# A state-space scan and a two-layer block on one Trainium2 core: reordering the first two pairs of chunks

## The chip, the cores and the metric

One core of a Trainium2 chip runs the whole program. The metric is device time in microseconds of one execution; lower is better. The span that a profile gives is some 1.7 us shorter than the time that is reported for the same execution (380.2 against 381.91 us for the profiled run of the kernel before); it runs from the first to the last instruction. All runs below were in the fast state, and all gave the correct result.

## The reference, cut to what matters

A selective state-space scan over 4 batches, 8 heads, 768 steps, 32 values and 16 states per head; its output, as 3072 tokens of 256 values, goes through two matrices with a leaky activation between them.

```python
# a clipped to [1e-6, 1]; the state runs from step to step of a sequence
M      = (C @ B.T) * causal * prod(a[j+1..i])     # inside a chunk
y      = M @ x + (C @ state) * prod(a[..i])       # "running products" of a
state  = prod(a) * state + B.T @ (x * prod(a[j+1..]))
# then, token by token
h = y @ w_in                                      # 256 -> 2048, 16 steps f of 128
g = max(h, 0) + alpha * min(h, 0)
out = g @ w_out                                   # weights come as float64
```

The weights arrive as 64-bit floats and are converted on the chip, tile by tile (512 KB raw each): ScalarE takes a part (`wt`, `wg`), GpSimd a limit on `wt`, VectorE two bit operations (`wr`), and GpSimd, or VectorE with it, the closing addition into `w_in` or `w_out`.

## The kernel before: the parts that the change touches

The kernel works on chunks of 128 steps in pairs (256 tokens). Pairs 0 and 1 are one group of 512 tokens. The first four hidden steps (f=0 to 3) of this group are done in halves, as soon as a pair is there; from f=4 on, all 512 tokens are there and the long steady stretch begins. An operation that waits holds those behind it on its engine: in the change SyncE waited 3.9 us for one transfer, until 11.76 us, and issued no other load in that time (below). To *spread* the decays is to have TensorE copy their rows to all 128 partitions. *Warming products* (`keep_warm`) are matmuls on a constant tile whose results nobody uses; they keep TensorE busy in a wait (in the kernel before, four of them, eight matmuls, take 1.73 us ahead of pair 1's output products).

```python
    # pair 0: decays z spread by TensorE, running products pf by VectorE
    if gp == 0:
        z = first_a(ap, nc.vector)
        ahead[0] = spread(z, 0)
        nc.vector.tensor_scalar(out=ap, in0=ap, ...)            # clamp
        pf = prep.tile([P, 2 * Q], F32, name="pf")
        for k in range(2):
            nc.vector.tensor_tensor_scan(out=pf[:, ks], data0=ap[:, ks], data1=zeros, ...)
    ...
    # the order of the loads on SyncE's queue
    load_next(2)                    # weight tiles 1 and 2
    held["pr"] = rows_scan(0)
    rows_out(0)                     # stores of the rows: z and pf
    load_next()                     # weight tile 3
    load_pair(1)
    load_second()                   # pair 1's running products
    load_next(3)                    # tiles 4 to 6
    load_pair(2)                    # with its spread decays, 2 x 512 KB
    # convert_next() issues the load of tile 7 and of the later ones
    ...
    prelus = [hidden_two(0, 0, spare())]        # f=0, 1, first 256 tokens
    convert_a(*pieces[2])                       # ScalarE's and GpSimd's part of tile 3
    convert_next()                              # closing addition of tile 2
    ssm(1)
    prelus.append(hidden_two(0, 2, bank(0)))    # f=2, 3: needs tile 2
    ...
    for f in range(FIRST):                      # second 256 tokens, one f at a time
        hidden(0, f, 2 * Q, 2 * Q)
        if f == 1:
            identity_bank()
        if f % 2:
            convert_next()
```

## Time and profile before

| | kernel before |
|---|---|
| time, median (range) at first | 381.88 us (381.42 to 383.98), 3 runs |
| time, medians in the five later sets of runs | 380.98 to 381.47 us |
| mean granted TensorE clock, profiled run | 0.998 |
| output products of pair 0 start | 15.67 us |
| hidden products of f=0 / f=2 start | 18.01 / 23.53 us |
| hidden products of f=4 (512 tokens) start | 34.64 us |
| VectorE starts its part of f=4 | 40.03 us |

The prediction, further down, reads the engine table, the busy time by stretch and the chain of work of this kernel. Three more readings of the same trace are used there: ScalarE's table load took 1.28 us, from 6.01 us; pair 1's Gram bank for GpSimd took a ScalarE copy of 0.61 us (at 23.44) and a GpSimd product of 1.27 us (at 24.95); and a DMA packet of 1 KB took 46 ns in the median (640 packets in the first 60 us), so 128 of them, spread over 16 engines, come to some 0.4 us (an estimate from this figure). Three lines of TensorE's timeline are added here, since the comparison rests on them. Columns: start and length in us, engine, source line, operation, output and inputs, shapes, count; in square brackets the idle time just before and what is taken to have ended it.

```profile
15.67 0.37 PE L579 MATMUL ss<-cd,sm 64*128 64x128 f32 x1
...
18.01 1.90 PE L620 MATMUL hp<-xT,w_in 128*128 128x256 f32 x8
...
23.53 1.99 PE L620 MATMUL bank<-xT,w_in 128*128 128x256 f32 x8 [0.87 <-POOL w_in L247]
```

The first is the start of pair 0's output products (`cd` is C times the running products, `sm` the masked state). The second is the first hidden product. The third, for f=2, waited 0.87 us for GpSimd's closing addition of the second weight tile; remember that wait.

### The profile page before, as it was taken

The numbers are of one execution on the slowest core, as the hardware profiler recorded it, in microseconds if no ns is written. First come the engines' busy times: TensorE is split into PE (matmuls) and PEld (weight loads), VectorE is DVE, ScalarE is ACT, GpSimd is POOL, SyncE is SP. The second block draws the span as 40 slices with busy tenths as digits, with TensorE's granted clock in tenths as the row PEclk, the third lists the DMA queues.
The fourth block names the chain that finished last, engine by engine and source line by source line (L and its number), as shares of the span: only waits on it lengthen the run. The fifth ranks groups of instructions, "written<-read, shape, count | busy, mean of one in ns | idle before, by whom it ended". The sixth has DMA issues, their size and how long they took to land.

```text
span 380.2 us, 6170 instructions
## 1 busy us (share of the span) xinstructions
PE 371.0 (98%) x2223; PEld 294.8 (78%) x2223; DVE 241.2 (63%) x462; ACT 178.0 (47%) x384; POOL 200.3 (53%) x210
## 2 busy tenths in 40 slices
PE   8998999999999999999999999999999999999995
PEld 7775566668888788788788788788788788888884
DVE  6994799968537637738737747637847644643363
ACT  2575765525354444454444445445435425553441
POOL 4565465778858744634645535455445356254511
PEclk9999999999999999999999999999999999999999
DMA  7989897721008701004603603703701001001003
GB/s 143 195 216 300 212 290 161 154 68 57 28 21 174 138 3 55 2 0 69 140 2 62 146 2 57 152 0 54 154 2 28 2 0 28 3 0 29 0 0 83
DMA packets 121877, 30.71 MB, mean 81 GB/s; under 512 B 93736, under 2 KB 117752, under 8 KB 121848
## 3 DMA queue, kind: packets, MB, share of 16 engines
q1 hardware_dynamic: 116736, 29.74, 35.1%
q10 hardware_dynamic: 5112, 0.59, 1.1%
q8 instruction: 17, 0.28, 0.3%
q14 instruction: 12, 0.10, 0.1%
HBM read 26.98 MB, written 3.34 MB: 80 GB/s over the span
## 4 chain that ended last, share of the span: by engine, by line
PE 85%; DVE 4%; DMA 4%; SPq 2%; ACT 1%; issue 1%; POOL 1%; ACTq 0%; POOLq 0%; DVEq 0%
PE hp L728 34%; PE bank L703 32%; PE bank L642 5%; PE hp L606 4%; PE ss L586 2%; PE ss L534 2%; DMA nat<-in_C_dram 2%; DMA raw<-in_moe_w_in_dram 2%; PE ss L579 1%; DVE dec L421 1%; PE ss L505 1%; PE hp L534 1%; PE ss L450 1%; SPq L158 1%; DVE wr L241 1%; SPq L156 1%
## 5 line engine op out<-in xcount | busy, mean ns | idle before, releaser
L771 POOL TENSOR_TENSOR gt<-gt 128x512 f32<-128x512 f32 x58 | 73.7, 1271 | 25.9 <-DVE gt L713 17.8
L703 PE MATMUL bank<-gt,w_out 128*128 128x256 f32 x320 | 82.4, 381 | 0.0
L713 DVE SCALAR_TENSOR_TENSOR gt<-hp,s_mul,gt 128x256 f32<-128x256 f32 x120 | 52.5, 479 | 41.5 <-ACT gt L711 40.7
L711 ACT ACTIVATE gt<-hp,s_alpha 128x256 f32<-128x256 f32 x120 | 50.3, 470 | 48.0 <-PE hp L728 37.3
L762 POOL TENSOR_TENSOR gt<-gt 128x512 f32<-128x512 f32 x20 | 25.4, 1272 | 86.7 <-DVE gt L713 86.7
L703 PEld LDWEIGHTS bank<-gt,w_out 128*128 128x128 f32 x320 | 60.2, 190 | 10.2 <-issue 2.3
L703 PE MATMUL bank<-gt,ws 128*128 128x256 f32 x240 | 61.4, 379 | 0.0
L703 PEld LDWEIGHTS bank<-gt,ws 128*128 128x128 f32 x240 | 45.1, 190 | 5.8
L421 DVE TENSOR_TENSOR_SCAN dec<-abc,bank 128x256 f32<-128x256 f32 x80 | 48.1, 660 | 0.0
L747 DVE TENSOR_TENSOR hp<-hp,u 128x512 f32<-128x512 f32 x20 | 14.0, 700 | 49.1 <-ACT u L745 49.1
L728 PE MATMUL hp<-xT,w_in 128*128 128x256 f32 x160 | 43.1, 392 | 0.2
L728 PE MATMUL hp<-xs,w_in 128*128 128x256 f32 x160 | 43.1, 392 | 0.1
L728 PE MATMUL hp<-xs,ws 128*128 128x256 f32 x160 | 41.1, 379 | 0.0
L736 ACT COPY m<-hp 128x512 f32<-128x512 f32 x20 | 11.7, 586 | 57.4 <-PE hp L728 52.9
L728 PEld LDWEIGHTS hp<-xT,w_in 128*128 128x128 f32 x160 | 28.7, 189 | 9.1 <-ACT hp L757 4.7
L728 PEld LDWEIGHTS hp<-xs,w_in 128*128 128x128 f32 x160 | 28.4, 189 | 8.8 <-issue 4.2
L728 PEld LDWEIGHTS hp<-xs,ws 128*128 128x128 f32 x160 | 30.4, 190 | 4.1
L642 PEld LDWEIGHTS bank<-w_out,gt 128*128 128x128 f32 x128 | 24.2, 190 | 8.9 <-issue 5.4
L642 PE MATMUL bank<-w_out,gt 128*128 128x256 f32 x128 | 30.8, 381 | 0.0
L606 PE MATMUL hp<-xT,w_in 128*128 128x512 f32 (+1 forms) x64 | 27.2, 553 | 1.3 <-DVE gt L610 1.0
L751 DVE TENSOR_TENSOR c<-hp,m 128x512 f32<-128x512 f32 x20 | 13.6, 682 | 19.2 <-PE hp L728 19.2
L745 ACT COPY u<-hp 128x512 f32<-128x512 f32 x20 | 11.7, 586 | 19.6 <-PE hp L728 18.4
(157 smaller groups left out, 547.0 us busy)
## 6 DMA issues: line engine op xcount, KB each, us to landing
abc<-z SPq DMA_DIRECT2D x20, 512.0 KB, 5.7
raw<-in_moe_w_in_dram SPq DMA_DIRECT2D x8, 512.0 KB, 5.4
raw<-in_moe_w_out_dram SPq DMA_DIRECT2D x8, 512.0 KB, 5.8
xt<-in_x_dram SPq DMA_DIRECT2D x24, 128.0 KB, 2.9
out_dram<-o_sb SPq DMA_DIRECT2D x32, 64.0 KB, 1.9
nat<-in_B_dram SPq DMA_DIRECT2D x22, 64.0 KB, 2.7
nat<-in_C_dram SPq DMA_DIRECT2D x22, 64.0 KB, 3.4
ap<-pf SPq DMA_DIRECT2D x11, 128.0 KB
```

The costliest lines, as they stand in the source:

```text
L421: nc.vector.tensor_tensor_scan(out=dv[:, k, hs], data0=abc[k][:, hs], data1=ident_p[0], initial=0.0, op0=ALU.mult, op1=ALU.add)
L606: nc.tensor.matmul(hp, w_in[:, k, f * P : (f + 1) * P], xts[g][:, k, t0 : t0 + nt], start=(k == 0), stop=(k == KC - 1))
L642: nc.tensor.matmul(pos[0][t // 2][:, t % 2], gt[:, t * Q : (t + 1) * Q], w_out[:, f], start=(f == 0 and t % 2 == 0), stop=(f == NF - 1), s ...
L703: nc.tensor.matmul(ms[g][i][:, h], w, blocks[g, z][n][:, p], start=(q == 0 and h == 0), stop=(q == NQ - 1), skip_group_check=True)
L711: nc.scalar.mul(o[:, p], h[:, p], s_alpha[:, fs[p]])
L713: nc.vector.scalar_tensor_tensor(out=o[:, p], in0=h[:, p], scalar=s_mul[:, fs[p]], in1=o[:, p], op0=ALU.mult, op1=ALU.max)
L728: nc.tensor.matmul(to[:, p], w(2 * z + p), b, start=start and p == 0, stop=True, skip_group_check=True)
L736: nc.scalar.copy(out=m1, in_=A)
L747: nc.vector.tensor_tensor(out=Y, in0=Y, in1=u2, op=ALU.add)
L751: nc.vector.tensor_tensor(out=c22, in0=A, in1=m5, op=ALU.add)
L762: nc.gpsimd.tensor_tensor(out=tc_, in0=g22, in1=g12, op=ALU.subtract)
L771: eng.tensor_tensor(out=o, in0=x0, in1=x1, op=ALU.subtract)
```

## The change

Its intent is to shorten the front: VectorE is relieved of the clamp and two scans of pair 0 (the running products come back by a load from the store that is made anyway), one of four banks of Gram products goes to GpSimd, the decays are spread before the rows' work, the second 256 tokens of f=0 to 3 are done two steps to a bank, and the weight tiles are loaded in twos between the pairs' loads.

```diff
@@ pair()
         if gp == 0:
             z = first_a(ap, nc.vector)
             ahead[0] = spread(z, 0)
-            nc.vector.tensor_scalar(out=ap, in0=ap, scalar1=1e-6, scalar2=1.0, ...)
-            pf = prep.tile([P, 2 * Q], F32, name="pf")
-            for k in range(2):
-                ...tensor_tensor_scan(out=pf[:, ks], data0=ap[:, ks], data1=zeros, ...)
+            ahead[1] = spread(z, 1, bank)
             loads["z", 1] = first_a(loads["a", 1], nc.gpsimd)
+            yield
+            pf = first_pf
+            turned = rows_turn(0, held.pop("pr"))
... (cut: tiles and warming products; half of pair 0's `cz` from ScalarE to
...  GpSimd; pair 1's second spread moved ahead of the hidden products of f=0)
         if gp == 0:
             gram = products_bc()
-            dps = added()
+            dps = added(spare())
             yield
+            c_decayed()                                # GpSimd
+            times(dec[:, :, :2], one_less(gram))       # ScalarE copy, GpSimd product
@@ rows_out()
-            nc.sync.dma_start(out=scratch[key, i], in_=t)
+            eng = nc.scalar if (key, i) == ("pf", 0) else nc.sync
+            eng.dma_start(out=scratch[key, i], in_=t)
@@ order of the loads
     load_next(2)
+    first_pf = prep.tile([P, 2 * Q], F32, name="pf")
+    rows_clamp(0)
+    ssm(0)
     held["pr"] = rows_scan(0)
     rows_out(0)
-    load_next()
+    load_products(0, first_pf)
     load_pair(1)
-    load_second()
-    load_next(3)
-    load_pair(2)
+    load_products(1, loads["p", 1][3])
+    load_next(2)
+    load_pair(2, False)
+    load_next(2)
+    load_spread(2, *divmod(4, CPB))
@@ order of the work
+    convert_a(*pieces[2])
+    convert_next(first=False)                  # tile 2's addition, still behind tile 3
     ssm(1)
-    prelus.append(hidden_two(0, 2, bank(0)))
+    convert_a(*pieces[3])
+    prelus.append(hidden_two(0, 2, 0, spare()))
...
-    for f in range(FIRST):
-        hidden(0, f, 2 * Q, 2 * Q)
-        if f == 1:
-            identity_bank()
-        if f % 2:
-            convert_next()
+    convert_next(first=False)
+    for rest in [hidden_two(0, f, 2 * Q, spare()) for f in range(0, FIRST, 2)]:
+        rest()
+    identity_bank()
+    convert_a(*pieces[5])
+    convert_next()
```

## The prediction

> **What bounds the kernel now.** I read the engine table, then busy time by stretch, then the chain of work that ended last. TensorE is busy 98% of the 380.2 us span:
>
> ```profile
> PE 371.0 (98%) x2223; PEld 294.8 (78%) x2223; DVE 241.2 (63%) x462; ACT 178.0 (47%) x384; POOL 200.3 (53%) x210
> ```
>
> The busy time by stretch puts PE at 99.94 of 100 us from 100 to 200 us and 99.86 from 200 to 300. The change touches only the first two pairs of chunks and the first four f-steps, which end at 34.6 us when the first 128x512 hidden product starts. So only the start can be shortened, and PE's idle time in the first 60 us (5.2 us in these stretches) bounds the gain loosely. Transfers by stretch:
>
> ```profile
> 8.00:13.00 5.00, 4.79 (x58) 3.58 (x59) 4.29 (x6) 3.54 (x9) 1.99 (x3) 1.00 1.03 331
> 13.00:16.00 3.00, 2.65 (x20) 1.97 (x18) 2.90 (x7) 0.77 (x2) 1.35 (x2) 1.00 0.67 84
> 16.00:24.00 8.00, 6.94 (x90) 5.18 (x87) 7.45 (x11) 6.13 (x13) 5.01 (x10) 1.00 1.03 260
> 24.00:29.00 5.00, 4.91 (x56) 3.85 (x54) 4.38 (x9) 2.28 (x6) 3.28 (x5) 1.00 0.69 86
> 29.00:40.00 11.00, 9.79 (x37) 6.57 (x38) 4.34 (x8) 7.20 (x17) 5.86 (x7) 1.00 1.02 325
> 40.00:60.00 20.00, 19.08 (x89) 12.15 (x87) 19.11 (x34) 13.28 (x23) 11.01 (x12) 1.00 0.85 233
> ```
>
> The last two columns are the busy share of the DMA engines and GB/s. DMA is saturated from 8 to 40 us but for two holes: 13 to 16 us loses 3 x 0.33 = 1.0 us, 24 to 29 us loses 5 x 0.31 = 1.55 us. From 40 to 60 us VectorE is the full engine (19.11 of 20). The chain says how these join:
>
> ```profile
> 10.13 3.28 SPq L158
> ...
> 13.45 1.63 SPq L156
> ...
> 15.12 2.68 DMA nat<-in_C_dram
> 17.80 0.04 issue
> 17.84 0.33 PE hp L450
> ...
> 22.21 1.28 POOL w_in L247
> ...
> 25.53 1.73 PE bank L256 x8
> ...
> 29.57 7.12 DMA raw<-in_moe_w_in_dram
> ```
>
> Pair 1's C arrives at 17.80 us, its conversion of weights ends at 23.49, four wasted warming products fill 1.73 us, and from 29.57 the chain leaves PE for a weight transfer: the seventh raw weight tile (call it raw7), which lands at 36.69. ScalarE waits for it in order, with the work of step f=4 behind it, and VectorE behind that:
>
> ```profile
> 36.77 0.68 ACT L213 ACTIVATE wt<-raw 128x512 f32<-128x512 f32 x1 [2.43 <-DMA raw<-in_moe_w_in_dram]
> 40.03 0.75 DVE L610 SCALAR_TENSOR_TENSOR gt<-hp,s_mul,gt 128x512 f32<-128x512 f32 x1 [3.57 <-ACT gt L609]
> ```
>
> From 40.03 VectorE has no gap until 50.4, where PE waits for it; after 61 us PE alone is the chain. So the end moves with VectorE's start at 40.03, that is with raw7, and PE's 5 us do not count in full.
>
> [...] the store of the decay rows (z), issued from SP at 7.51 us behind two 512 KB weight tiles, has its landing event only at 11.87, against a median of 2.3 us for such stores.
> [...] The granted clock here is 1.00 in every stretch[...].
>
> **The change part by part.**
>
> *Spread ahead of the rows.* VectorE now clamps `ap` right after the rows' clamp instead of after two scans; `ap` has its landing event at 3.76 us, so z is ready near 4.25 instead of 5.17. Seven warming products instead of ten end at 1.23 + 14 x 0.217 = 4.3 us. The spread starts near 4.65 instead of 5.80. VectorE's first decay scan follows 1.5 us later, as now: 6.15 instead of 7.30. The four scans take 4 x 1.15 us and end near 10.8 instead of 12.19. *Gain so far 1.35 us.*
>
> *Running products by a load.* VectorE loses a clamp and two scans (0.29 + 0.89 us). In return the products make a round trip through DRAM. The store moves to ScalarE's queue, where it waits for nat C (7.43 us), ahead of the table load. It lands near 9.2 to 9.8 (2.3 us for such a store). The load of 128 KB follows behind the two weight tiles and lands near 12.6. Two costs: the table load no longer fills idle time but runs 7.9 to 9.2, then two copies, so `bc` ends at 10.2 instead of 9.36; and GpSimd's `cd` waits until 12.6 instead of running at 9.44.
>
> *Gram bank by GpSimd.* VectorE loses 0.65 us, ScalarE gains a 0.61 copy, GpSimd 1.27. GpSimd then runs `cd` 12.6 to 13.3, the product to 14.7, the mask to 15.4 (0.73 each for first and last). VectorE, with the first weight conversion (0.41 + 0.69) moved forward, ends its last gram near 15.0. So pair 0's output products start near 15.6, now 15.67: *the 1.35 us is spent on GpSimd's chain, nothing is left of it here.*
>
> *Pair 1.* Its loads go out behind two weight tiles instead of three, and C should land near 16.7 instead of 17.80. Transposes 17.0 to 18.0; spread to 19.2 (now after the hidden products); hidden_two to 20.95; sums and grams to 22.9. GpSimd ends the second weight conversion near 24.1, because ScalarE reaches the third tile's part later (now 23.49): hidden_two 24.15 to 26.0. Two warming products instead of four save 0.86 us; output products 26.9 to 28.35, now 27.25 to 28.73. *Gain 0.35 us.*
>
> *Tokens two to a bank.* Now eight products of 128x256 run from 29.18 to 34.64 through two buffers, each waiting for ScalarE and VectorE: 5.46 us, of which PE needs about 3.6 and the transposes 0.6. In pairs they should need 28.8 to 33.0. *Gain 1.3 us more, 1.65 in all at step f=4.*
>
> *Loads reordered.* Before raw7 the same bytes move as now, plus the 128 KB (0.4 us: 128 packets x 50 ns / 16 engines). What changes are the holes. Now SP is blocked for 3.28, 1.63, 2.28, 3.15 and 1.54 us at small transfers behind three weight tiles, and issues the next ones after DMA has run dry. With tiles in twos the small transfers go out while the tiles still run. If both holes (2.5 us) close and 0.4 + 0.4 us (product load, round trip) are added, raw7 lands near 36.7 - 2.5 + 0.8 = 35.0; if half closes, near 36.2. ScalarE itself, by its order, is free for raw7 near 34.8 (pair products until 32.6, a bank copy 0.38, the sixth tile 1.8).
>
> *Sum.* VectorE starts f=4 near 35.0 + 3.3 instead of 40.03: -1.7 us; PE is ready for it by -1.65. Behind it the order on all engines is unchanged, so the end moves by -1.6 us; half-closed holes give -0.5.
>
> **The rivals.**
> (A) *DMA keeps raw7 where it is.* For it: 1.02 of share from 29 to 40 us, the same bytes, and one weight tile fewer ahead of pair 1, so one more after. Against: the holes. Time then 381.5 to 382.3; PE would reach f=4 early and stand at f=6.
> (B) *GpSimd's chain in pair 0 or the third weight tile is worse than I think.* The product load is a new wait, and ScalarE needs the third tile near 21.5, while it lands near 20. Two microseconds late there would make 382 to 383.
> (C) *The front gains more.* If the product load lands by 11.5, pair 0 gains another 1 us and, holes closed, VectorE's start moves by 2.5 us or more: 378.5 to 379.5.
> (D) *PE falls to half clock* with fewer warming products. The first matmul of 0.58 us against 0.27 later hints at it; PE is fuller than now, so I give it little.
>
> **Range and chances.** Centre 381.9 - 1.6 = 380.3 us. (A) and (B) together bound it above near 382.0, (C) below near 378.5; I take these as the 8 in 10. A 2% change is 7.6 us, more than all of PE's idle time in the front, so faster by 2% is nearly out. Slower by 2% would need a stall of over 7 us, which no wait I found approaches. Chances 0.02, 0.97, 0.01.
>
> **What would show it.** First decay scan near 6.2 us and the fourth ending near 10.8 (step 1). `cd` of pair 0 waiting for DMA until about 12.6, and pair 0's output products still near 15.6. Hidden_two for f=2 starting near 24. First 128x512 hidden product near 33.0 (now 34.6). ScalarE's wait for raw7 ending near 35.0 and VectorE's gap ending near 38.3; DMA share above 0.9 in 13 to 16 and 24 to 29 us. From 61 us on all stretches as now, only shifted. I am wrong if raw7 lands at 36.5 or later and the total is still shorter (then the chain through it is no bound), or if the front moves by 3 us and the end by none.

## The result, and the profile after

The changed kernel took 386.59 us in the median of 4 runs (385.79 to 388.11), the kernel before 382.00 of 4 runs (381.42 to 383.98). The ratio is 1.0121, with a 95% interval from 1.0075 to 1.0167. Ratios here and below are the mean time of one kernel's fast runs over that of the other's fast runs of the same rounds, so not quite the ratio of the quoted medians. The change makes the kernel 1.2% slower; 380.3 us had been predicted, in a range from 378.5 to 382.0, and the measured median lies 4.6 us above the top of the range.

The page of the changed kernel already shows one difference. Each digit of this line is the granted TensorE clock of one fortieth of the span, in tenths; it was 9 throughout before.

```profile
PEclk9879999999999999999999999999999999999999
```

The busy time by stretch, with the stretches of the prediction. Columns: stretch, its length, busy time (and count) of PE, PEld, DVE, ACT and POOL, granted clock, DMA share, GB/s.

```profile
8.00:13.00 5.00, 4.67 (x49) 3.69 (x51) 4.49 (x6) 4.35 (x10) 2.21 (x3) 1.00 0.64 211
13.00:16.00 3.00, 1.80 (x18) 1.23 (x14) 2.20 (x5) 1.11 (x2) 1.08 (x2) 1.00 0.73 108
16.00:24.00 8.00, 6.22 (x57) 4.88 (x58) 5.27 (x6) 2.24 (x5) 5.22 (x10) 0.58 0.98 217
24.00:29.00 5.00, 3.37 (x32) 2.31 (x30) 4.12 (x7) 3.19 (x7) 1.91 (x4) 1.00 0.87 132
```

From 16 to 24 us the clock was 0.58: half speed from 17.22 to 24.05 us, and TensorE was nearly as busy as before (6.22 against 6.94 us) for far fewer matmuls (57 against 90). From 8 to 13 us DMA fell from a share of 1.03 to 0.64. Two waits lie behind both. The chain of work of the changed kernel (start, length, what):

```profile
12.23 2.65 issue
...
14.92 0.45 POOL cd L486
...
15.60 1.26 POOL dec L568
16.86 0.87 POOL sm L542
...
17.77 0.58 PE ss L609
```

GpSimd's `cd` could start only at 14.92 us; its product and its mask follow in order; and the output products of pair 0 start at 17.77 us, not at 15.67. What `cd` and TensorE waited for is in their timelines (first GpSimd, then TensorE):

```profile
14.92 0.72 POOL L486 TENSOR_TENSOR cd<-bc,pf 128x256 f32<-128x256 f32 x1 [2.69 <-DMA pf<-pf]
```

```profile
17.77 0.58 PE L609 MATMUL ss<-cd,sm 64*128 64x128 f32 x1 [2.97 <-POOL sm L542]
```

The load of the running products landed at 14.84 us. It was issued at 11.76 us, when the store had landed (11.75), and SyncE had issued nothing since 7.78 us, with all loads of pair 1 still to come. This is the longest of SyncE's own waits (us in total, times, longest):

```profile
SPq L176 <- DMA pf<-rpf: 3.9, 1, 3.9
```

So one round trip costs three things: 2.10 us on GpSimd's chain, a hole of 3.9 us in the issue of loads, and a gap of 2.97 us on TensorE (14.80 to 17.77 us), in which the clock fell to half (at 17.22). At half clock the first product took 0.58 us here, at full clock 0.37 in the kernel before.

Taken point by point, in us from the start:

| | before | predicted | change |
|---|---|---|---|
| first decay scan | 7.30 | 6.15 | 6.63 |
| fourth decay scan ends | 12.19 | 10.8 | 11.20 |
| load of the running products lands | none | 12.6 | 14.84 |
| pair 0's output products start | 15.67 | 15.6 | 17.77 |
| hidden products of f=0 start | 18.01 | - | 23.42 |
| hidden products of f=2 start | 23.53 | 24.15 | 29.31 |
| hidden products of f=4 start | 34.64 | 33.0 | 38.09 |
| seventh weight tile lands (last of its landing events) | 36.69 | 35.0 | 38.62 |
| VectorE starts f=4 | 40.03 | 38.3 | 43.75 |
| span | 380.2 | - | 384.1 |

VectorE's start moved by 3.72 us and the span by 3.9: the loss lies ahead of that start. The span less that start is 340.17 us before and 340.35 after; in all 17 profiles of this study it lies between 340.1 and 341.3.

In the changed kernel nobody waits for the seventh tile any more. ScalarE comes to it late, with its own work in a row:

```profile
38.59 0.38 ACT L333 COPY bank<-ident_h 128x256 f32<-128x256 f32 x1
38.89 0.68 ACT L218 ACTIVATE wt<-raw 128x512 f32<-128x512 f32 x1
39.46 1.15 ACT L228 ACTIVATE wg<-raw,g_add,g_mul 128x256 f32<-128x256 uint16 x2
40.49 0.68 ACT L218 ACTIVATE wt<-raw 128x512 f32<-128x512 f32 x1
```

The reader is to see no bracket in the last line: the seventh tile is there when ScalarE reaches it, 1.9 us after its last landing event at 38.62 us.

### The profile page after: what moved, and what is told of

It is laid out like the page before. It is cut to its first block, busy times and chain, and to the rows that moved or that the text cites. A ratio compares the mean times of both kernels' runs of the same rounds, so it can differ in the third digit from the quotient of the medians.

```text
span 384.1 us, 6169 instructions
## 1 busy us (share of the span) xinstructions
PE 371.9 (97%) x2221; PEld 296.1 (77%) x2221; DVE 241.3 (63%) x458; ACT 178.0 (46%) x384; POOL 202.5 (53%) x212
## 3 DMA queue, kind: packets, MB, share of 16 engines
q1 hardware_dynamic: 116760, 29.82, 35.4%
## 4 chain that ended last, share of the span: by engine, by line
PE 87%; DVE 5%; ACT 3%; issue 2%; ACTq 1%; POOL 1%; DMA 1%; POOLq 0%; DVEq 0%
PE hp L759 34%; PE bank L734 31%; PE bank L673 5%; PE hp L635 3%; PE ss L616 3%; PE hp L650 2%; PE ss L556 2%; PE ss L609 1%; DVE dec L440 1%; PE ss L527 1%; PE hp L556 1%; PE ss L466 1%; DVE wr L239 1%; DMA nat<-in_C_dram 1%; DVE gt L639 1%
## 5 line engine op out<-in xcount | busy, mean ns | idle before, releaser
L635 PE MATMUL hp<-xT,w_in 128*128 128x512 f32 x48 | 23.2, 605 | 0.0
```

The source lines that it names most:

```text
L635: nc.tensor.matmul(hp, w_in[:, k, f * P : (f + 1) * P], xts[g][:, k], start=(k == 0), stop=(k == KC - 1))
```

## The experiments

The first theory was that the products' round trip is the cause, through its wait and the half clock. Its rivals were the order of the loads, the order of the conversions, and that the half clock is only a sign of waiting. Each set of runs has its own runs of the kernel before on the same chip (medians 381.23, 380.98, 381.19, 381.47 and 381.36 us), and each ratio is to those.

| run | what is different | ratio (95%) | median us | VectorE starts f=4 |
|---|---|---|---|---|
| change | | 1.0121 (1.0075 to 1.0167) | 386.59 | 43.75 |
| E1 | change, products by VectorE | 1.0087 (1.0061 to 1.0113) | 384.35 | 41.90 |
| E2 | change, gap at pair 0 filled | 1.0111 (1.0091 to 1.0131) | 385.28 | 42.75 |
| E3 | change, tiles 1, 2 behind the round trip | 1.0127 (1.0104 to 1.0150) | 386.07 | 44.61 |
| E4 | before, second tokens two to a bank | 0.9998 (0.9982 to 1.0013) | 381.34 | 39.14 |
| E5 | E1, old loads | 1.0029 (1.0017 to 1.0042) | 382.33 | 40.66 |
| E6 | E1, conversions swapped | 1.0084 (1.0053 to 1.0116) | 384.45 | 38.88 |
| E7 | E1, old loads and conversions swapped | 1.0007 (0.9997 to 1.0017) | 381.21 | 38.77 |
| E8 | change, old loads and conversions swapped | 1.0062 (1.0043 to 1.0082) | 383.07 | 41.04 |
| E9 | before, tile 7 ahead of pair 2's spread decays | 0.9987 (0.9969 to 1.0005) | 380.28 | 37.78 |
| E10 | E7, tile 7 first, tile 6 earlier on ScalarE | 0.9926 (0.9900 to 0.9952) | 378.33 | 35.78 |
| E11 | E4, tile 7 first, tile 6 earlier on ScalarE | 0.9952 (0.9937 to 0.9968) | 379.47 | 37.41 |
| E12 | change, old loads | 1.0119 (1.0088 to 1.0151) | 385.63 | 43.65 |
| E13 | change, conversions swapped | 1.0103 (1.0076 to 1.0131) | 385.02 | 42.23 |
| E14 | change, both gaps filled | 1.0123 (1.0088 to 1.0157) | 385.86 | 43.65 |
| E15 | change, old loads and the gap at pair 0 filled | 1.0079 (1.0057 to 1.0100) | 384.32 | 41.45 |

Two cautions go with this table. The ratio of the change comes from 4 runs and is known to some 0.5% only. E5, E7 and E8 are clear of it; the single repairs E1, E2, E3, E12 and E13, and E14, E6 and E15, are not told from it by the timed ratio alone, so for these the traces carry the argument. And each start in the last column is from one execution. The traced one of the kernel before took 381.91 us, 0.4 to 0.9 us above the later medians; with 1.7 us off for the span and 340.2 us after the start, those medians put its usual start near 39.1 to 39.6 us (an estimate), not at 40.03.

### E1: the products by VectorE again

```diff
-    load_products(0, first_pf)
+    first_ap = loads["p", 0][3]
+    nc.vector.tensor_scalar(out=first_ap, in0=first_ap, scalar1=1e-6, scalar2=1.0, ...)
+    for k in range(2):
+        ...tensor_tensor_scan(out=first_pf[:, ks], data0=first_ap[:, ks], data1=zeros, ...)
```

> The changed kernel with one thing undone: VectorE forms pair 0's running products again (a clamp and two scans, 1.2 us, placed in its gap before the first decay scan), so nothing of pair 0 waits for the round trip through DRAM; the store stays on ScalarE's queue and pair 1 still loads its products. If the wait for the loaded products is the cause (theory W), pair 0's output products start near 15.2 us instead of 17.8, PE's idle stretch of 3 us before them is under 0.7 us, the clock is never granted at half from 17 to 24 us, step f=4 starts near 33 us instead of 38.1 and the kernel takes 379.5 to 381.5 us, at least 5 us less than the change. If the new order of the loads or the gram bank on GpSimd is the cause, it stays at 384 us or more.

Pair 0's output products started at 16.02 us (17.77 in the change), and there was no half clock at 17 us. Yet the time was 1.0087: about a quarter of the loss came back, if any (the intervals overlap), and the expected 5 us did not. ScalarE's timeline shows a new wait, for the fifth weight tile, with the copies of pair 1's output (`xT`) behind it, for which the second tokens' hidden products wait:

```profile
30.69 0.68 ACT L218 ACTIVATE wt<-raw 128x512 f32<-128x512 f32 x1 [1.43 <-DMA raw<-in_moe_w_in_dram]
31.27 0.66 ACT L225 ACTIVATE wg<-raw 128x512 f32<-128x512 uint16 x1
31.82 0.37 ACT L623 COPY xT<-bank 128x256 f32<-128x256 f32 x1
```

In the old order the fifth tile goes out ahead of pair 2's loads, in the new one behind them. In the change it landed at 31.47 us and ScalarE reached it at 32.07, so the wait was hidden by only 0.6 us.

### E2: the gap at pair 0 filled with warming products

```diff
-            keep_warm(y[0].rearrange("p k t -> p (k t)"), 2)
+            keep_warm(y[0].rearrange("p k t -> p (k t)"), 8 if gp == 0 else 2)
```

> The changed kernel with eight warming products instead of two ahead of pair 0's output products, which fill PE's idle stretch while the products are on their way. The wait stays, so the output products still start near 17.8 us. If the half clock from 17.2 to 24.0 us is a cause of its own (theory C), it goes away and PE gets back up to half of these 6.8 us: output products 0.9 us, transposes 0.5, spread 1.1, hidden_two 0.3: 2.8 us, so about 384 us. If the clock costs nothing at the end, the time stays within 0.5 us of the change.

The fill worked where it stood: no half clock from 17 to 24 us, and the hidden products of f=0 began at 20.92 instead of 23.42 us, though pair 0's output products began at 17.81 as in the change. But the clock then fell at the end of the next gap (1.94 us), ahead of f=2, and was half from 26.4 to 29.8 us, and ScalarE waited 0.49 us for the fifth tile. VectorE's start moved by 1.0 us of the 2.5 won earlier.

### E3: the first two weight tiles issued after the round trip

```diff
-    load_next(2)
     first_pf = prep.tile([P, 2 * Q], F32, name="pf")
     ...
     load_products(0, first_pf)
+    load_next(2)
```

> The changed kernel with the first two weight tiles issued after the load of pair 0's products instead of ahead of its store. If the store of the products, though on ScalarE's queue, is held up by the weight tiles ahead of it on SP's queue (theory Q), it lands near 9.5 us instead of 11.75, the products land near 12 instead of 14.84, pair 0's output products start near 15.5 to 16.5 and the clock stays full. DMA loses some 2 us at the start, so raw7 lands 1 to 2 us later than in the change (38 to 39); in all 382 to 385 us. If the store is slow by itself (a fixed 4.4 us round trip), it lands at 11.7 all the same and the time is no better than the change.

The product load was issued at 8.64 instead of 11.76 us and GpSimd no longer waited for it. Pair 0's output products still started at 17.82. ScalarE now waited 3.18 us for the first weight tile, until 13.17, and GpSimd's part of that tile stands ahead of `cd` in its queue, which started at 14.62. The wait was exchanged for another of the same length. This run missed as a remedy, but it shows the store alone: 2.6 us, from 6.07 to 8.62 us, with no weights issued ahead of it, against 4.46 us in the change (7.29 to 11.75), where 1 MB of weights had been issued first. There the store is on ScalarE's queue and the two tiles are on SyncE's; from 8.0 to 10.5 us the DMA view of the change lists 402 packets, all of q1, which by its 29.82 MB is SyncE's (ScalarE's, q10, moved 0.64 MB in the whole run), and the store landed when the second tile was all but there (12.06). Why it waited is not shown.

### E4: only the second tokens two to a bank, in the kernel before

```diff
-    for f in range(FIRST):
-        hidden(0, f, 2 * Q, 2 * Q)
-        ...
+    convert_next(first=False)
+    for rest in [hidden_two(0, f, 2 * Q, spare()) for f in range(0, FIRST, 2)]:
+        rest()
+    identity_bank()
+    convert_a(*pieces[5])
+    convert_next()
```

> The kernel before with one part of the change alone: the last 256 tokens of the first four f-steps go two to a bank. If raw7 (landing at 36.7 us) bounds what follows, as I predicted, step f=4 starts near 33.3 instead of 34.6 us but VectorE's first product of f=4 stays near 40.0, and the whole gains under 0.8 us: 381.0 to 382.0. If PE bounds instead, all of the 1.3 us comes through: 380.6.

TensorE reached f=4 at 33.47 instead of 34.64 us, and the time did not change (0.9998). The loop of the kernel before had ScalarE's copy of the identity (0.38 us) and its part of the sixth tile (1.8 us) between the hidden products; now they stand behind them. ScalarE reached the seventh tile at 35.86 us and did not wait for it (it had landed at 34.71): ScalarE's own work had taken the place of the wait.

### E5, E6, E7: the order of loads and of conversions, beside E1

```diff
  E5 and E7
     load_products(0, first_pf)            # E1: by VectorE
+    load_next()
     load_pair(1)
     load_products(1, loads["p", 1][3])
-    load_next(2)
-    load_pair(2, False)
-    load_next(2)
-    load_spread(2, *divmod(4, CPB))
+    load_next(3)
+    load_pair(2)
  E6 and E7
-    convert_a(*pieces[2])
     convert_next(first=False)
+    convert_a(*pieces[2])
```

> The first experiment's kernel (VectorE forms pair 0's products) with the order of the loads of before: the third weight tile ahead of pair 1, the next three ahead of pair 2. In the first experiment ScalarE stands 1.4 us for the fifth weight tile, which lands at 30.6 us, with pair 1's copies of the tokens behind it. If the new order of the loads is that cost (theory L), the fifth tile lands before 27 us, ScalarE no longer waits for it and the kernel gains 1.0 to 1.5 us on the first experiment (384.35): 382.9 to 383.3. If the order of the loads does not matter, it stays at 384.4. PE's second gap, 22.8 to 24.7 us, and the half clock after it stay.

> The first experiment's kernel with the second weight tile's conversion finished ahead of the start of the third's, as before the change, so that GpSimd's addition for it does not stand behind ScalarE. If that order makes PE's second gap (theory G: PE waits 2.3 us for w_in from GpSimd until 24.7), hidden_two for f=2 starts near 23 us and no half clock is granted from 24.9 us. The gain at the end is small as long as ScalarE waits for the fifth tile until 30.6 us: 383.5 to 384.3. If the gap and the half clock set the end by themselves, 2.5 us or more are gained: 381.8 or less.

> Both of the last two edits together on the first experiment's kernel. If the three costs (products' round trip, order of the loads, order of the conversions) are all there is, no half clock is granted after 10 us, step f=4 starts at 32.5 to 34 us (34.6 before the change) and the time is that of the kernel before within 1 us: 380.5 to 382. If something else of the change costs, such as the gram bank on GpSimd, it stays over 383.

With the products by VectorE, the old loads are worth 1.0087 - 1.0029 = 0.6% without the swap and 1.0084 - 1.0007 = 0.8% with it. The swap is worth 0.2% with the old loads and nothing that can be told with the new ones. E7, with all three undone, is level with the kernel before. So what is left of the change in E7 (the spread ahead of the rows, the Gram bank on GpSimd, two to a bank) neither costs nor gains; it starts f=4 on TensorE 2.3 us earlier (32.38 us), and ScalarE then waits 0.62 us for the seventh tile, which bounds the kernel before as well.

E6 was the odd one. The same program took 381.19, 382.47, 386.38, 384.08, 385.39, 384.81, 382.91 and 385.85 us, at mean clocks of 1.000, 0.999, 0.991, 0.996, 0.991, 0.995, 0.996 and 0.991. Its profiled run happened to be the fastest, with no half clock, so its early VectorE start in the table is not its usual one. The slow executions are those with the low clock. Reckoned from the mean clock of 0.991 and a span of 380 us, at most 0.009 x 380 = 3.4 us of TensorE time were lost (an estimate), and those three executions are 4.2 to 5.2 us slower than the first, so the lost clock is not all of the difference, unless the shift brings new waits. At full clock, on the other hand, the traced execution is level with E7 (381.19 and 381.21 us) though it has the new loads.

### E8: old loads and swapped conversions, the round trip kept

> The changed kernel with the old order of loads and of conversions, but with the products' round trip kept. If the round trip alone costs as much as the whole (theory W), pair 0's output products still start at 17.8 us or later (the third weight tile is now ahead of nothing of pair 0, so the same), the half clock from 17 to 21 us or longer stays and the time is 384 to 386. If the costs do not add but the last one decides, because the fourth to seventh tiles come earlier again, it is 382 to 383.

The edit is that of E7 without E1's part. At 1.0062 it lies 0.55% above E7, about 2.1 us, for the round trip alone. In its profiled run the clock stayed full until 43 us, so it helps to separate the waits from the clock: from pair 0's output products to the hidden products of f=0 took 20.37 - 17.26 = 3.11 us, against 5.65 in the change and 2.34 before. In that interval the half clock costs 5.65 - 3.11 = 2.54 us; E2, which differs from the change by the fill alone, gives the same 3.11 (20.92 - 17.81). The rest, 3.11 - 2.34 = 0.77, is put down to the spread of pair 1 moved ahead of the hidden products. The round trip reached the end by another way here, through SyncE: all loads come later, and the seventh tile landed at 37.7 us instead of 35.4 in E7 (in whose traced execution the first tile had been issued 0.83 us earlier), and ScalarE waited for it:

```profile
37.80 0.66 ACT L218 ACTIVATE wt<-raw 128x512 f32<-128x512 f32 x1 [2.42 <-DMA raw<-in_moe_w_in_dram]
```

### E12 and E13: the loads alone, the conversions alone

The edits are those of E5 and E6 without E1's part.

> The change with only the old order of loads: three weight tiles ahead of the second pair, three after it, the third pair's loads in one piece. If the three costs add up (round trip of the products, order of loads, order of conversions), the order of loads is worth 0.6 to 0.8% as it was beside products on VectorE, so the ratio is 1.004 to 1.006. If the third tile ahead of the second pair makes the product load land later and eats the gain, 1.010 or more. In the trace the fifth tile should land before 27 us instead of 31.5, and the half clock at 17.2 us, which follows the wait for the products, should stay.

> The change with only the order of the conversions swapped: GpSimd's addition for the second weight tile ahead of its part of the third. If the addition standing behind ScalarE's late work is what holds the hidden products of f=2, they start some 4 us after those of f=0 instead of 5.9 (25.3 to 27.5 us against 29.31), VectorE starts f=4 2 us earlier at most, and the ratio is 1.007 to 1.010. If the fifth weight tile, which lands near 31.5 us in this order of loads, then holds ScalarE instead, the start of f=4 moves by less than 0.5 us and the ratio stays at 1.011 to 1.013.

E12 missed: the costs do not add up. The old loads, worth 0.6 to 0.8% beside E1, win nothing that can be told while the round trip is there (1.0119). Pair 0's output products came at 17.75 us, the half clock from there on as in the change, and VectorE's start at 43.65. E13 (1.0103) can't be told from the change by its time, but shows what TensorE's wait before f=2 really is. GpSimd's timeline in the change:

```profile
27.29 0.61 POOL L220 TENSOR_SCALAR wt<-wt 128x512 f32<-128x512 f32 x1 [3.01 <-ACT wt L218]
27.98 1.28 POOL L261 TENSOR_TENSOR w_in<-wr,wg 128x512 uint32<-128x512 uint32 x1
```

The second line is the closing addition of the second tile, which f=2 needs. It ends at 29.26, and f=2 starts at 29.31. It stands behind the limit on the third tile, which waits for ScalarE. With the two swapped, f=2 started 3.6 us after f=0 (26.11 after 22.52 us) instead of 5.9, though TensorE's wait had been put down to VectorE. Then the fifth tile took most of it back:

```profile
31.03 0.67 ACT L218 ACTIVATE wt<-raw 128x512 f32<-128x512 f32 x1 [1.65 <-DMA raw<-in_moe_w_in_dram]
```

Beside the old loads, which bring that tile earlier, the swap is worth more: E8 lies 0.57% below E12.

### E14 and E15: is the half clock a cost of its own?

E14 is E2 with eight warming products ahead of f=2 as well; E15 is E12 with the fill of E2.

```diff
  E14
         ts = slice(t0, t0 + nt)
+        if (f, t0) == (2, 0):
+            keep_warm(hp, 8)
```

> The change with TensorE's two long gaps filled with warming products: eight instead of two ahead of the first pair's output products (as in the earlier run with a warm fill, 1.0111) and eight ahead of the hidden products of f=2, where that run went to half clock from 26.4 us. No wait is changed. If the half clock is a cost of its own, no window of half clock is left before 40 us, the hidden products of f=2 take 2.0 instead of 3.6 us, VectorE starts f=4 near 41.2 (42.75 with one fill, 43.75 in the change), and the ratio is 1.005 to 1.008; the rest is what the waits cost at full clock. If the half clock only fills time that PE would wait anyway, VectorE's start stays at 42.5 or later and the ratio at 1.010 or more.

> The change with the old order of loads (alone 1.0119) and the gap ahead of the first pair's output products filled with eight warming products (alone 1.0111). Reading to be tested: the half clock and the late fifth weight tile run side by side, so taking away one leaves the time where it was. Then with both gone the gain shows: the hidden products of f=0 start near 20.9 instead of 23.4 us, no fifth tile is waited for, VectorE starts f=4 near 41 instead of 43.65, and the ratio is 1.004 to 1.008. If the half clock costs nothing of itself, the ratio stays at 1.010 or more.

E14 kept the clock at 1.000 for the whole run and was no faster (1.0123). It is not a clean test: the eight products took 3.5 us, twice what I had reckoned, and f=2 started at 28.01 us, later than in E2 (26.52). And the fifth tile was waited for:

```profile
32.46 0.67 ACT L218 ACTIVATE wt<-raw 128x512 f32<-128x512 f32 x1 [1.69 <-DMA raw<-in_moe_w_in_dram]
```

E15 is the cleaner one. It differs from E12 by six warming products alone, which lie inside a wait. (In its traced execution pair 0's output products also came 0.72 us earlier, at 17.03 instead of 17.75 us, as the loads were issued earlier.) The stretch from 16 to 24 us, in E12 and then in E15 (columns as above):

```profile
16.00:24.00 8.00, 6.25 (x58) 4.96 (x59) 5.27 (x6) 2.24 (x5) 4.82 (x8) 0.57 0.94 205
```

```profile
16.00:24.00 8.00, 7.64 (x89) 5.57 (x91) 6.73 (x9) 3.20 (x8) 4.79 (x11) 1.00 0.92 216
```

The clock is 1.00 instead of 0.57, and TensorE gets 89 matmuls done instead of 58 (5 of the 89 are warming products). VectorE's start moved from 43.65 to 41.45 us, of which 0.72 us was there before, and the ratio from 1.0119 to 1.0079. Both say about 1.5 us for the half clock once the late fifth tile does not cover it; the timed difference, 0.40%, is only just outside the noise (the two intervals overlap a little). In the change the tile does cover it: E2 takes away the half clock there and wins little, E12 takes away the late tile and wins nothing, E15 takes away both.

When does the half clock come? The length of the gaps does not tell. In the profiled runs, gaps of TensorE of 2.97 us in the change, 2.92 in E12, 3.11 in E13 and 1.94 in E1 and E2 were followed by half clock, while 2.63 in E8 and 1.94 in E15, and later gaps of 1.94 in the change and in E12 (to 29.31 and 29.21 us), were not.

The traces say more than that. In the change the granted clock was full from 6.98 us (its first entry), half from 17.22, full again from 24.05 and half from 382.45: stretches of 10.24, 6.83 and 358.40 us, that is 3, 2 and 105 times 3.413. In the kernel before, the first stretch, from 6.48 us, lasted 372.05 us, 109 times 3.413, and in E1, E2 and E13 the half clock lasted some 3.4 us. Cut these traces into steps of 3.41 us from the first entry and take the share of a step in which TensorE had a matmul. Up to 40 us, the falls to half clock followed steps busy to 0.29 in the change, 0.15 in E13, at most 0.35 in E12, 0.43 in E1 and 0.46 in E2. In the kernel before, no step up to 33.79 us was busy to less than 0.75, and no fall came. But two steps, busy to 0.46 in the change (from 27.46 us) and 0.43 in E12 (from 27.28 us), were not followed by a fall, so no rule can be read from this. The gap of the change lies mostly in one step (0.99 us busy of 3.41), that of E8, nearly as long and followed by no half clock, is split over two:

```profile
13.81:17.22 3.41, 0.99 (x4) 0.54 (x4) 2.61 (x5) 0.30 (x1) 2.30 (x3) 1.00 0.97 112
```

```profile
12.37:15.79 3.42, 2.26 (x22) 1.65 (x20) 2.96 (x6) 1.53 (x4) 1.39 (x2) 1.00 0.86 222
15.79:19.20 3.41, 1.94 (x40) 1.55 (x40) 3.41 (x4) 0.59 (x2) 3.25 (x5) 1.00 1.05 131
```

The first entry comes at 4.70 us in E13, 6.48 in the kernel before and 6.98 in the change, so the steps lie differently in each execution. Whether that explains the spread of E6 (381.19 to 386.38 us, at clocks from 1.000 down to 0.991) is not shown, as only one execution of E6 was traced.

### E9, E10, E11: what the front is worth when its end is opened

E9 tests the prediction's claim that the seventh tile bounds the kernel before. E10 and E11 add that ScalarE's part of the sixth tile and its copy of the identity move into a hole of 1.81 us ahead of the paired products.

```diff
  E9, E10, E11
-    load_pair(2)
+    load_pair(2, False)                       # without its spread decays
     ...
     convert_next(halves=(nc.vector, nc.gpsimd))   # issues the load of tile 7
+    load_spread(2, *divmod(4, CPB))
  E10 (from E7) and E11 (from E4)
     convert_next(first=False)
+    identity_bank()
+    convert_a(*pieces[5])
     for rest in [hidden_two(0, f, 2 * Q, spare()) for f in range(0, FIRST, 2)]:
         rest()
-    identity_bank()
-    convert_a(*pieces[5])
     convert_next()
```

> The kernel before, with one edit: the two 512 KB loads of the third pair's spread decays go out after the seventh raw weight tile instead of ahead of it. Theory (VectorE's start of f=4 sets the end; in the ten traces so far the span less that start lies between 340.2 and 340.7 us, and in the kernel before the seventh tile sets that start): the tile lands near 33.5 instead of 36.69 us, ScalarE takes it at 34.3 without a wait, VectorE starts f=4 near 37.6 instead of 40.03, the span is near 378, and the timed ratio to the kernel before is 0.994 to 0.997. Rival (the bound only seems to be there: a later wait, for the spread decays or for GpSimd's additions, takes it back by 50 us): the tile lands earlier, the start moves, but span less start grows by as much, and the ratio is 0.999 to 1.001.

> The version with products on VectorE, old loads and conversions swapped (1.0007 of the kernel before), with two edits: the seventh raw weight tile ahead of the third pair's spread decays, and ScalarE's part of the sixth tile and its copy of the identity into a bank put ahead of the two groups of paired products, where ScalarE idles 1.81 us. Theory: ScalarE is through with the paired products near 33.0, the seventh tile is there by 32.5, VectorE starts f=4 near 36.4 instead of 38.77, ratio 0.993 to 0.996; the first version that beats both kernels. Rival (the front is worth nothing whatever is done): 0.999 to 1.001. A third way: the sixth tile's work delays the paired products' release by over 0.5 us and the gain halves, 0.997.

> The kernel before with only the second-half tokens two to a bank (0.9998 of the kernel before) and the same two edits as in the run before this one. Theory: VectorE starts f=4 near 37.2 instead of 39.14, ratio 0.994 to 0.997, and what it loses to the run before this one, 0.7 us or less, is all that the earlier spread and the GpSimd gram bank are worth. Rival: 0.999 to 1.001.

In E9 the wait for the seventh tile is gone and VectorE starts f=4 at 37.78, 2.25 us earlier, but the span less that start grew from 340.2 to 341.2 us, and the timed gain of 0.13% can't be told from zero: the rival of the expectation came nearer than its theory. (One of its 14 runs, 384.00 us at a clock of 0.991, pulls the mean up; its median is 0.9 us below.) After 34.94 us the chain of work no longer goes through VectorE but through TensorE, in a row that is unbroken up to 49 us:

```profile
34.94 1.96 PE hp L611 x4
36.89 1.73 PE bank L647 x8
```

So with the tile early, TensorE's own arrival at f=4 is the next bound, and there the paired products, which the change brings, do count. E11 has them, on top of the kernel before, and reaches 0.9952. E10 has the rest of the change as well and reaches 0.9926, 378.33 us in the median (377.77 to 379.26): the fastest version here, 2.9 us below the kernel before in the same set. Its ScalarE timeline:

```profile
27.46 0.40 ACT L333 COPY bank<-ident_h 128x256 f32<-128x256 f32 x1
27.78 0.69 ACT L218 ACTIVATE wt<-raw 128x512 f32<-128x512 f32 x1
29.24 1.14 ACT L228 ACTIVATE wg<-raw,g_add,g_mul 128x256 f32<-128x256 uint16 x2 [0.78 <-POOL w_in L261]
30.29 1.66 ACT L656 ACTIVATE gt<-hp,s_alpha 128x256 f32<-128x256 f32 x4
32.52 0.68 ACT L218 ACTIVATE wt<-raw 128x512 f32<-128x512 f32 x1 [0.57 <-DMA raw<-in_moe_w_in_dram]
```

The sixth tile's part now lies ahead of the paired products' activation (`gt`), and the seventh tile is begun at 32.52 us, before at 36.77. What the rest of the change gains is the difference between E11 and E10, 0.26% or about 1 us; their intervals just overlap.

## Why the prediction was wrong

- **What bounds the end.** Right. The end moves with VectorE's start of f=4: the span less that start was 340.1 to 341.3 us in every profile. E9 marks its limit: once that start comes 2 us earlier, TensorE takes over for 1 us of it.
- **Spread ahead of the rows.** Right in kind; gain 1.0 us instead of 1.35 (the fourth scan ended at 11.20 us, not at 10.8). The difference goes with the clock's first entry: in all 13 traces with this spread it began at 4.49 to 4.52 us, but the first scan came at 5.79 (E13, first full clock granted at 4.70) to 6.63 us (the change, 6.98). In the change most spreading matmuls ahead of 6.18 us took 0.42 us, in the kernel before 0.27 from 6.55 us on, where the first entry is at 6.48.
- **Products by a load: the step that failed first.** "It lands near 9.2 to 9.8 (2.3 us for such a store)" and "lands near 12.6". The store took from 7.29 to about 11.75 us behind 1 MB of weights, and the load landed at 14.84. The time of a store was taken from its median, which in that view stands for a single store, issued at 58.81 us, though the same prediction had just shown a store needing 4.4 us behind the same two tiles; from ScalarE's queue, to which it had moved, the store still landed only when the second tile was all but there (12.06). That SyncE stood still meanwhile (3.9 us), with every later load behind it, was not reckoned at all; in E8, which differs from E7 by the round trip alone, the seventh tile came 2.3 us later.
- **Pair 0's output products at 15.6 us.** Wrong by 2.2 us, which is the lateness of the load. GpSimd's chain behind it was sized well: 2.85 us from `cd` to the products, 3.0 predicted.
- **The clock, rival (D), "so I give it little".** Wrong. The gap of 2.97 us was followed by half clock for 6.8 us. E2 and E8 put this at 2.5 us between two points of the chain, and E12 with E15 at about 1.5 us at VectorE's start. The reason given, that TensorE is fuller than now, did not hold: it was busy for 0.99 us of the 3.41 before the fall.
- **Loads reordered.** Wrong: pair 1's C landed at 18.01 us instead of 16.7, the third tile at 21.94 instead of 20, the seventh at 38.62 instead of 35.0, later than before the change. And the step did not follow the fifth tile, which the new order puts behind pair 2's loads. E1, E13 and E14 show ScalarE waiting for it for 1.43 to 1.69 us. The holes did not close either: the DMA share from 13 to 16 us was 0.73, and the stretch from 8 to 13 fell to 0.64.
- **Tokens two to a bank.** Right: from f=2 to f=4 took 38.09 - 29.31 = 8.78 us, and 33.0 - 24.15 = 8.85 had been predicted. But it won nothing at the end in E4, since ScalarE's 2.2 us of work moved behind it; this was not seen.
- **The sum.** VectorE's start moved by +3.72 us instead of -1.7: output products of pair 0 +2.10, from there to f=0 +3.31 (half clock 2.54, spread 0.77), f=0 to f=2 +0.37, f=2 to f=4 -2.33, f=4 to VectorE +0.27. Rival (B) had named a product load two microseconds late, but at 382 to 383 us; it lacked the clock and the fifth tile. One reading was off without consequence: the 5.2 us of idle TensorE "in these stretches" are 3.84 in the six lines shown, and 5.07 with the first 8 us.

The causes run side by side and mask each other, which is why single repairs gave at most 0.3%, within the noise of the change's own ratio, and all three (E7) 1.1%. What stays open: why the half clock follows one gap and not another, and how much of the front's loss in the timed runs of the change was clock in each of them, since only one of its executions was traced.

## What to carry to other kernels

Here the store of a round trip through DRAM took 4.5 us with 1 MB of weights issued ahead of it, instead of 2.6, and the engine that waited for it issued no later load for 3.9 us; size such a trip from a transfer in the same place, not from a median. When a repair wins nothing, look for a second wait that ends at nearly the same time (here 0.6 us of slack on one weight tile) before you call the first one harmless. And before an engine is relieved, find the instruction whose start moves the end, and clear the queue in front of that one first: here this was worth 0.7%, after the rest of the change had been worth nothing.
